# The head of a one-core S5 + SwiGLU kernel: other warm-up operands, a first tile in halves, reordered gate quarters, later parameter transposes

## The chip, the core and the metric

The kernel runs on one core of one Trainium2 chip. The metric is the device time of an execution in microseconds. The engines are called as in the profile: PE is TensorE (matmuls; PEld its weight loads), DVE is VectorE, ACT is ScalarE, POOL is GpSimd, SP is SyncE, which issues nearly all DMAs here. L712 means line 712 of the kernel before.

## The reference

For x of shape (1, 2048, 512) in bfloat16:

```python
xn = layernorm(x)                                  # over the last axis, eps 1e-5
# A: a diagonal complex state space model with 512 states
dt = exp(log_dt); Lam_bar = exp(dt * (Lambda_re + 1j * Lambda_im))
Bu = xn @ (((Lam_bar - 1) / Lam)[:, None] * B).T
h[t] = Lam_bar * h[t - 1] + Bu[t]                  # 2048 steps
y = 2 * real(h @ C.T) + xn * Dskip
# B: a feed-forward layer of width 1376
f = (silu(xn @ w_gate) * (xn @ w_up)) @ w_down
out = x + y + f
```

## The kernel before

The 2048 rows of x are 16 tiles of 128 rows; four tiles make a chunk, and there are four chunks. For each chunk the kernel normalizes the tiles (bn_stats, bn_aggr and the addition of eps on DVE, rstd by a power on POOL, and the scaling on DVE for chunks 0 and 1, on ACT for 2 and 3), transposes them into xnT so that the features lie on the partitions, and then runs matmuls: gate and up projections of the feed-forward layer in 11 column tiles of 128 (the last has 96), the B projection of the state space model, and at the end the down projection together with C and the Dskip term in one PSUM accumulation. The recurrence is turned into a real scan on DVE by tables of sines and cosines, which ACT and DVE make once in the head (`tables`, lines 635 to 649) from the parameters (`params_a`, `params_b`).

Only the head matters here. Tiles 0 to 3 are transposed on PE (`xt_tile_fine`, L523) and copied from PSUM to xnT by ACT (L529). Each of the other chunks is transposed by a DMA. So that PE can start before all four tiles are there, chunk 0's first six gate tiles are computed in quarters (`ffn_gate_quarters`, L712): for each row tile q four matmuls of 128 columns for each of the six gate tiles, 24 per quarter, and all six results stay in PSUM until the four quarters are done. After that come the up projections (L684) in matmuls of 512 columns.

In front of that PE runs ten warm-up matmuls of 512 columns on a tile of zeros, `zt`, which POOL sets (`pe_warm`, L451, L442), and four small transposes that bring the four parameter rows (`prow`) onto the partitions (`params_t`, L460). DVE copies the result to `praw` (L463); from it POOL computes dt as a power (L586), DVE the angle thn (L588), and ACT the first table step tm (L635), after which the sine tables follow.

What sets the order: the kernel lists its steps as tasks with what they read and write, and `_schedule` writes down a fixed order for each engine before anything runs. On PE and SP the order is that in which the tasks were added. On DVE, ACT and POOL it is a list scheduler with estimated durations (`est`): of the tasks that could begin within 200 ns of the earliest, it takes the one with the longest remaining path, plus a task's `prio`. `_plan` and `_emit` then put semaphore waits in front of the instructions; an engine runs its list strictly in order. Dependences follow the tasks' reads and writes, a later writer of a buffer waiting for its readers too.

The eight PSUM banks are handed out in a circle by `next_bank`; a bank is skipped only if PE wrote it last and no reader has been listed yet:

```python
def _bank_live(b):
    lw = g.last_w.get(("bk", b, 0))
    rd = g.readers.get(("bk", b, 0), ())
    return lw is not None and lw.eng == "pe" and len(rd) == 0 and not lw.name.startswith("pe_warm")
```

The loads go out on SP in the order x0, x1, x2 with x3, wgA (gate tiles 0 to 2), wg0 (gate tiles 3 to 5), wu0, wg1, wu1, x4 to x7. The four parameter rows are loaded on ACT's queue.

Of the kernel before, what the change touches and what calls it, by code (L numbers as in the profile page):

```python
# [21 lines left out]
    warm=10,  # L22
# [8 lines left out]
class _Task:  # L31
    __slots__ = ("eng", "fn", "deps", "name", "est", "idx", "dma", "sem", "lvl",
                 "waits", "nsig", "vc", "out", "lat", "bl", "start", "fin", "nbytes", "prio", "ninst")
# [5 lines left out]
class _Graph:  # L39
# [5 lines left out]
    def add(self, eng, fn, reads=(), writes=(), name="", est=100.0, dma=False, after=(), out=False, nbytes=0, prio=0.0, ninst=1):  # L45
        t = _Task()
        t.eng, t.fn, t.name, t.est, t.dma, t.out, t.nbytes, t.prio = eng, fn, name, float(est), dma, out, nbytes, prio
        t.ninst = ninst
        t.idx = len(self.tasks)
        deps = set(after)  # L50
        for r in reads:
            w = self.last_w.get(r)
            if w is not None:
                deps.add(w)
        for r in writes:
            w = self.last_w.get(r)
            if w is not None:
                deps.add(w)
            for rd in self.readers.get(r, ()):
                deps.add(rd)  # L60
        for r in reads:
            self.readers[r].append(t)
        for r in writes:
            self.last_w[r] = t
            self.readers[r] = []
        deps.discard(t)
        t.deps = deps
        t.sem = None
        t.lvl = 0
        t.lat = 0.0  # L70
        self.tasks.append(t)
        return t
# [8 lines left out]
def _schedule(tasks, engines, slack=200.0):  # L81
    succ = defaultdict(list)
    for t in tasks:
        for d in t.deps:
            succ[d].append(t)
    chain_next = {}
# [6 lines left out]
    for t in reversed(tasks):  # L93
        b = 0.0
        for s in succ[t]:
            if s.bl > b:
                b = s.bl
        v = b + t.est + t.lat
        cn = chain_next.get(t)
        if cn is not None and cn.bl + t.est > v:  # L100
            v = cn.bl + t.est
        t.bl = v + t.prio
    remaining = {e: [t for t in tasks if t.eng == e] for e in engines}
    nun = {t: len(t.deps) for t in tasks}
# [135 lines left out]
def bass_parallel_sum__ssm_conv_s5__swiglu_ffn__prompt_kernel(  # L240
# [32 lines left out]
    with es:  # L273
        block = es.enter_context(nc.Block())

        def sb(name, shape, dt):
            return es.enter_context(nc.sbuf_tensor(name, shape, dt))
# [48 lines left out]
        zt = sb("zt", [128, 512], B16)  # L326
# [80 lines left out]
        pload("ld_dskp", 3, A_Dskip)  # L407
        dma("ld_x0", x_sb[:, 0:1, :], x_v[:, 0:1, :], [("x", 0)], TILEB)
        dma("ld_x1", x_sb[:, 1:2, :], x_v[:, 1:2, :], [("x", 1)], TILEB)
        dma("ld_x2", x_sb[:, 2:4, :], x_v[:, 2:4, :], [("x", 2), ("x", 3)], 2 * TILEB)  # L410
        FQ = 3 * 128
        dma("ld_wgA", wg[:, :, 0:FQ], wg_v[:, :, 0:FQ], [("wg", "a")], 512 * FQ * 2)
        dma("ld_wg0", wg[:, :, FQ:FH0], wg_v[:, :, FQ:FH0], [("wg", 0)], 512 * (FH0 - FQ) * 2)
# [28 lines left out]
        g.add("pool", lambda e: e.memset(zt[:], 0.0), writes=[("zt",)], name="zt", est=450)  # L442
# [3 lines left out]
        def pe_warm(n):  # L446
            bk = next_bank()

            def mm(e, bk=bk):
                for _ in range(n):  # L450
                    inst = e.matmul(pbank[:, bk, :], lhsT=zt[:, 0:128], rhs=zt[:], start=True, stop=True)  # L451
                return inst
            g.add("pe", mm, reads=[("zt",)], writes=BK(bk), name="pe_warm", est=n * 430, ninst=n)

        def params_t():
            slot = next_tr()

            def tr(e, slot=slot):
                for k in range(4):
                    inst = e.transpose(out=ptr[:, slot, 4 * k:4 * k + 4], in_=prow[0:4, k, :], identity=ident[0:4, 0:4])  # L460
                return inst
            g.add("pe", tr, reads=[("prow", k) for k in range(4)] + [("ident",)], writes=BK(slot), name="parT", est=400, ninst=4)
            g.add("dve", lambda e, slot=slot: e.tensor_copy(out=praw[:].rearrange("p k a -> p (k a)"), in_=ptr[:, slot, 0:16]),  # L463
                  reads=BK(slot), writes=[("praw", k) for k in range(4)], name="parTev", est=80, prio=5000.0)
            for kt in range(KT):
                g.add("dve", lambda e, kt=kt: e.tensor_scalar(out=diagD[:, kt, :], in0=ident[:], scalar1=praw[:, 3, kt:kt + 1], scalar2=None, op0=ALU.mult),
                      reads=[("praw", 3), ("ident",)], writes=[("diagD", kt)], name="diagD%d" % kt, est=90)

        ln_prev = [None]
        ln_xn = {}  # L470

        def ln_tile(a, norm_act):
            g.add("dve", lambda e, a=a: e.bn_stats(out=st[:, a, :], in_=x_sb[:, a, :]),  # L473
                  reads=[("x", a)], writes=[("st", a)], name="bnst%d" % a, est=640,
                  after=(((ln_prev[0],) if (ln_prev[0] is not None and a < 4) else ()) + ((ln_xn[a - 2],) if (a < 4 and (a - 2) in ln_xn) else ())))
            g.add("dve", lambda e, a=a: e.bn_aggr(out=mv[:, a, :], in_=st[:, a, :]),
                  reads=[("st", a)], writes=[("mv", a)], name="bnag%d" % a, est=90)
            ln_prev[0] = g.add("dve", lambda e, a=a: e.tensor_scalar(out=ve[:, a:a + 1], in0=mv[:, a, 1:2], scalar1=EPS, scalar2=None, op0=ALU.add),  # L478
                                reads=[("mv", a)], writes=[("ve", a)], name="ve%d" % a, est=70)
            g.add("pool", lambda e, a=a: e.tensor_tensor(out=rstd[:, a:a + 1], in0=ve[:, a:a + 1], in1=mhalf[:, a:a + 1], op=ALU.pow),  # L480
                  reads=[("ve", a), ("mhalf",)], writes=[("rstd", a)], name="rstd%d" % a, est=400)
# [4 lines left out]
            else:  # L486
# [3 lines left out]
                      reads=[("x", a), ("rstd", a), ("nmr", a)], writes=[("xn", a % NXN)], name="xn%d" % a, est=710)  # L490

# [4 lines left out]
        def xt_chunk(c):  # L496
            a0 = 4 * c
            for pair in range(2):
# [12 lines left out]
                def evac(e, aa=aa, slot=slot):  # L511
# [3 lines left out]
                      writes=[("xnT", c % 2, aa % 4), ("xnT", c % 2, aa % 4 + 1)], name="xTev%d" % aa, est=930)  # L515

        def xt_tile_fine(c, a):
            if True:
                slot = next_tr()

                def tr4(e, a=a, slot=slot):
                    for kt in range(KT):
                        inst = e.transpose(out=ptr[:, slot, kt * 128:(kt + 1) * 128],  # L523
                                           in_=xn_sb[:, a % NXN, kt * 128:(kt + 1) * 128], identity=ident[:])
                    return inst
                g.add("pe", tr4, reads=[("xn", a % NXN), ("ident",)], writes=BK(slot), name="xT%d" % a, est=4 * 64, ninst=4)

                def evac(e, a=a, slot=slot):
                    return e.activation(out=xnT[:, c % 2, a % 4, :, :],  # L529
                                        in_=ptr[:, slot, 0:512].rearrange("p (k t) -> p k t", k=KT), func=AF.Identity)  # L530
                g.add("act", evac, reads=BK(slot), writes=[("xnT", c % 2, a % 4)], name="xTev%d" % a, est=500)

        def xt_chunk_dma(c):
            s0 = (4 * c) % NXN
            dma("xTd%d" % c, xnT[:, c % 2].rearrange("p j k t -> p (j k) t"), xn_sb[:, s0:s0 + 4, :],
                [("xnT", c % 2, j) for j in range(4)], 4 * TILEB, reads=[("xn", s0 + j) for j in range(4)], xpose=True)
# [140 lines left out]
        def ffn_mm(c, i, which):  # L677
# [9 lines left out]
            g.add("pe", mm, reads=[wres("wg" if which == "g" else "wu", i)] + [("xnT", c % 2, j) for j in range(4)],  # L687
# [12 lines left out]
        def ffn_gate_quarters(c, tiles):  # L700
            xt_tile_fine(c, 4 * c)
            banks = {i: next_bank() for i in tiles}
            for q in range(4):
                for ii, i in enumerate(tiles):
                    if q < 3 and ii == 0:
                        xt_tile_fine(c, 4 * c + q + 1)
                    fs = fsz[i]
                    bk = banks[i]

                    def mm(e, bk=bk, i=i, fs=fs, c=c, q=q):  # L710
                        for kt in range(KT):
                            inst = e.matmul(pbank[0:fs, bk, q * 128:(q + 1) * 128], lhsT=wg[:, kt, i * 128:i * 128 + fs], rhs=xnT[:, c % 2, q, kt, :],  # L712
                                            start=(kt == 0), stop=(kt == KT - 1))
                        return inst
                    g.add("pe", mm, reads=[wres("wg", i), ("xnT", c % 2, q)], writes=BK(bk), name="mm_gq%d_%d_%d" % (c, i, q), est=4 * 62, ninst=4)
# [29 lines left out]
        def ssm_b_unit(c, pt):  # L745
            br, bi = next_bank(), next_bank()
            for ri, bk in ((0, br), (1, bi)):
# [5 lines left out]
                g.add("pe", mm, reads=[("BT", ri, kt) for kt in range(KT)] + [("xnT", c % 2, j) for j in range(4)],  # L753
# [66 lines left out]
        def dc_chunk(c, mid=None, split_last=False):  # L820
# [10 lines left out]
            for (lt, c0, nc_), bk in zip(items, banks):  # L831
# [11 lines left out]
                g.add("pe", mmA, reads=[("hT", hb, i) for i in range(FT)] + [("wd", 0), ("wd", 1)] + ([("xnT", c % 2, lt)] + [("diagD", kt) for kt in range(KT)] if dg else []),  # L843
# [27 lines left out]
        ln_chunk(0)  # L871
        params_t()
# [7 lines left out]
        ffn_gate_quarters(0, [0, 1, 2, 3, 4, 5])  # L880
# [93 lines left out]
```

## Time and profile before

| | us |
|---|---|
| median of 3 runs | 183.49 (183.48 to 183.89) |
| span of the profiled execution, first to last instruction | 181.8 |
| median less span, what lies around it | 1.69 |
| PE busy | 177.7 (98% of the span) |
| DVE busy | 165.0 (91%) |
| ACT busy | 91.4 (50%) |
| POOL busy | 13.4 (7%) |

The profile gives the profiled execution by its span; its own time is taken as that span and the 1.69 us that separate the span from the median of the runs. The spans are of one execution. A row of the chain of waits or of the timeline gives the start, the length, the engine, the line, and in the timeline the operation, out<-in by the program's names, shapes, a count, and in brackets the idle time before it and what ended that. Matmuls are pipelined: their lengths overlap, and the distance of their starts is what one costs in a row.

### The profile page before, as it was taken

What the parts mean: (1) busy time and instruction counts of PE and PEld (TensorE: products, weight loads), DVE (VectorE), ACT (ScalarE), POOL (GpSimd) and SP (SyncE); (2) the same over time, 40 slices, a digit from 0 to 9 for tenths busy, and PEclk for the clock granted to TensorE, in tenths of its full rate; (3) what the DMA queues carried; (4) which work ended last, traced back from release to release, by engine and by line L of the source; (5) the groups of instructions that cost most, each with busy time, mean ns of one, the idle gap of its engine ahead of it and who ended that gap; (6) DMA issues with size and microseconds to landing.
All of it is one profiled execution on the core that took longest, in us unless ns stands there. A gap on an engine that the chain in (4) does not pass through costs nothing.

```text
span 181.8 us, 2579 instructions
## 1 busy us (share of the span) xinstructions
PE 177.7 (98%) x937; PEld 86.8 (48%) x937; DVE 165.0 (91%) x359; ACT 91.4 (50%) x162; POOL 13.4 (7%) x30
## 2 busy tenths in 40 slices
PE   6999999999999999999999999999999999999994
PEld 2694444444444454444444455444444444444643
DVE  3899878999999998999999999999999999999733
ACT  3299989996899108057666380026677620000000
POOL 5530500000000013000000220000000000000000
DMA  5992666669100000730000000620000000000102
GB/s 146 325 375 61 141 130 108 145 182 346 49 0 4 0 0 0 128 108 0 0 0 0 0 4 0 115 94 22 0 4 2 2 0 0 0 32 29 58 29 87
DMA packets 23388, 12.39 MB, mean 68 GB/s; under 512 B 15088, under 2 KB 23376, under 8 KB 23376
## 3 DMA queue, kind: packets, MB, share of 16 engines
q1 hardware_dynamic: 23344, 12.23, 25.3%
q8 instruction: 7, 0.11, 0.3%
q14 instruction: 5, 0.04, 0.1%
q10 hardware_dynamic: 32, 0.00, 0.0%
HBM read 6.46 MB, written 2.10 MB: 47 GB/s over the span
## 4 chain that ended last, share of the span: by engine, by line
PE 97%; ACT 0%; POOL 0%; DVE 0%; issue 0%; DVEq 0%; POOLq 0%
PE pb L684 39%; PE pb L838 21%; PE pb L854 15%; PE pb L750 15%; PE pb L712 3%; PE pb L451 2%; PE pb L841 1%; PE pb L523 1%; ACT xnT L529 0%; POOL zt L442 0%; DVE osb L865 0%; PE pb L460 0%; POOL mhalf L432 0%; DVEq L234 0%; POOLq L959 0%
## 5 line engine op out<-in xcount | busy, mean ns | idle before, releaser
L684 PE MATMUL pb<-xnT,wu 128*128 128x512 bf16 (+1 forms) x176 | 43.7, 379 | 0.0
L838 PE MATMUL pb<-wd,hT 128*128 128x512 bf16 (+3 forms) x187 | 39.7, 367 | 0.0
L789 DVE TENSOR_TENSOR_SCAN vq<-sm,car,vq 128x512 bf16<-128x512 f32 x32 | 39.5, 1271 | 0.1
L684 PE MATMUL pb<-xnT,wg 128*128 128x512 bf16 (+1 forms) x152 | 38.4, 379 | 0.0
L734 ACT ACTIVATE uf<-pb 128x512 bf16<-128x512 f32 (+1 forms) x44 | 25.4, 603 | 6.8 <-PE pb L684 6.6
L854 PE MATMUL pb<-W,hss 128*128 128x512 bf16 (+1 forms) x136 | 28.3, 366 | 0.0
L750 PE MATMUL pb<-xnT,BT 128*128 128x512 bf16 x128 | 28.1, 379 | 0.0
L684 PEld LDWEIGHTS pb<-xnT,wu 128*128 128x128 bf16 (+1 forms) x176 | 17.6, 100 | 20.1
L838 PEld LDWEIGHTS pb<-wd,hT 128*128 128x128 bf16 (+1 forms) x187 | 18.0, 98 | 18.5
L697 ACT ACTIVATE sg<-pb 128x512 bf16<-128x512 f32 (+1 forms) x38 | 22.5, 597 | 7.5 <-PE pb L684 7.4
L684 PEld LDWEIGHTS pb<-xnT,wg 128*128 128x128 bf16 (+1 forms) x152 | 15.3, 100 | 17.6
L757 ACT ACTIVATE u_sb<-pb 128x512 bf16<-128x512 f32 x16 | 9.6, 600 | 20.5 <-PE pb L750 20.3
L854 PEld LDWEIGHTS pb<-W,hss 128*128 128x128 bf16 x136 | 13.2, 98 | 13.9
L750 PEld LDWEIGHTS pb<-xnT,BT 128*128 128x128 bf16 x128 | 12.5, 98 | 15.1
L736 DVE TENSOR_TENSOR hT<-sg,uf 128x512 bf16<-128x512 bf16 (+1 forms) x44 | 18.1, 416 | 1.2 <-ACT uf L734 0.7
L480 POOL TENSOR_TENSOR rstd<-ve,mhalf 128x1 f32<-128x1 f32 x16 | 9.4, 604 | 90.4 <-DVE ve L478 90.4
L473 DVE BATCH_NORM_STATS2 st<-x_sb 128x6 f32<-128x512 bf16 x16 | 10.4, 685 | 2.9 <-DMA x_sb<-in_A_x_dram 2.8
L780 DVE TENSOR_TENSOR scrA<-u_sb,cosT 128x1024 bf16<-128x1024 bf16 x16 | 10.9, 682 | 0.7 <-ACT u_sb L759 0.7
L489 ACT ACTIVATE xn_sb<-x_sb,nmr,rstd 128x512 bf16<-128x512 bf16 x8 | 5.9, 803 | 10.2 <-POOL rstd L480 8.8
L799 DVE TENSOR_TENSOR scrA<-vq,sin 128x1024 bf16<-128x1024 bf16 x16 | 11.0, 684 | 0.0
L783 DVE TENSOR_TENSOR scrA<-u_sb,sin 128x1024 bf16<-128x1024 bf16 x16 | 10.9, 684 | 0.0
L795 DVE TENSOR_TENSOR scrA<-vq,cosT 128x1024 bf16<-128x1024 bf16 x16 | 10.9, 684 | 0.0
(71 smaller groups left out, 135.8 us busy)
## 6 DMA issues: line engine op xcount, KB each, us to landing
out_dram<-osb SPq DMA_DIRECT2D x15, 128.0 KB, 1.7
x_sb<-in_A_x_dram SPq DMA_DIRECT2D x3, 512.0 KB, 7.6
wd<-in_B_w_down_dram SPq DMA_DIRECT2D x1, 1280.0 KB, 7.0
wg<-in_B_w_gate_dram SPq DMA_DIRECT2D x2, 384.0 KB, 4.6
wu<-in_B_w_up_dram SPq DMA_DIRECT2D x1, 768.0 KB, 7.4
wg<-in_B_w_gate_dram SPq DMA_DIRECT2D x1, 608.0 KB, 8.5
wu<-in_B_w_up_dram SPq DMA_DIRECT2D x1, 608.0 KB, 9.6
x_sb<-in_A_x_dram SPq DMA_DIRECT2D x2, 128.0 KB, 2.2
```

Of the source, the lines that this page charges most:

```text
L684: inst = e.matmul(pbank[0:fs, bk, :].rearrange("p (j t) -> p j t", j=4), lhsT=w[:, kt, i * 128:i * 128 + fs], rhs=xnT[:, c % 2, :, kt, :], ...
L697: g.add("act", lambda e, sl=sl, bk=bk, fs=fs: e.activation(out=sg[0:fs, sl, :], in_=pbank[0:fs, bk, :], func=AF.Silu), reads=BK(bk), write ...
L734: g.add("act", lambda e, ul=ul, bk=bk, fs=fs: e.activation(out=uf[0:fs, ul, :], in_=pbank[0:fs, bk, :], func=AF.Identity), reads=BK(bk), w ...
L736: g.add("dve", lambda e, sl=sl, ul=ul, fs=fs, i=i, hb=hb: e.tensor_tensor(out=hT[0:fs, hb, i, :], in0=sg[0:fs, sl, :], in1=uf[0:fs, ul, :] ...
L750: inst = e.matmul(pbank[:, bk, :].rearrange("p (j t) -> p j t", j=4), lhsT=BT[:, ri, kt, pt * 128:(pt + 1) * 128], rhs=xnT[:, c % 2, :, kt ...
L780: g.add("dve", lambda e, sl=sl, U=U, Cb=Cb: e.tensor_tensor(out=pr2[:, sl, 0], in0=U, in1=Cb, op=ALU.mult), reads=ru + rdt, writes=[("pr", ...
L783: g.add("dve", lambda e, sl=sl, Usw=Usw, S2=S2: e.tensor_tensor(out=pr2[:, sl, 1], in0=Usw, in1=S2, op=ALU.mult), reads=ru + rdt, writes=[ ...
L789: g.add("dve", lambda e, sl=sl, ri=ri, pt=pt, rr=rr, c=c: e.tensor_tensor_scan(out=vq[:, sl, 1, ri, :], data0=rr[:, pt:pt + 1].to_broadcas ...
L795: g.add("dve", lambda e, sl=sl, Q=Q, Cb=Cb: e.tensor_tensor(out=po2[:, sl, 0], in0=Q, in1=Cb, op=ALU.mult), reads=rq + rdt, writes=[("po", ...
L799: g.add("dve", lambda e, sl=sl, Qsw=Qsw, S2sw=S2sw: e.tensor_tensor(out=po2[:, sl, 1], in0=Qsw, in1=S2sw, op=ALU.mult), reads=rq + rdt, wr ...
L838: inst = e.matmul(pbank[:, bk, 0:nc_], lhsT=hT[0:fs, hb, i, lt * 128:(lt + 1) * 128], rhs=wd[0:fs, i, c0:c0 + nc_], start=(i == 0), stop=F ...
L854: inst = e.matmul(pbank[:, bk, 0:nc_], lhsT=hss[:, hb, pt, ri, lt * 128:(lt + 1) * 128], rhs=W12[:, ri, pt, c0:c0 + nc_], start=False, sto ...
```

## The change

The warm-ups are nine and read a constant of ones (bfloat16) that the program's header sets on POOL in any case; `zt` and its memset are gone. x2 and x3 are loaded apart, x3 after wgA. The four parameter transposes are split into three (k = 0, 1, 2) and one (k = 3, Dskip, with diagD behind it) and stand inside the gate quarters. Tile 0 is transposed and copied in two halves of two transposes each, in two banks, and its first three gate tiles are computed in two halves to match. Three small matmuls (`pe_fill`) are put in front of them. The quarters run in another order, with gate tiles 0 to 2 (A) and 3 to 5 (B) apart. The order of the layer norm on DVE for tiles 0 to 3 is written out by hand in `ln_head` as order-only dependences (`order`, `odeps`), which the scheduler honours without a semaphore; rstd of the first four tiles has a higher `prio` and a larger `est`. `XN(c, j)` names the two halves of a transposed tile, `XNC(c)` all of a chunk. The computation is the same.

```diff
-    warm=10,
+    warm=9,
...
-        dma("ld_x2", x_sb[:, 2:4, :], x_v[:, 2:4, :], [("x", 2), ("x", 3)], 2 * TILEB)
+        dma("ld_x2", x_sb[:, 2:3, :], x_v[:, 2:3, :], [("x", 2)], TILEB)
         dma("ld_wgA", wg[:, :, 0:FQ], wg_v[:, :, 0:FQ], [("wg", "a")], 512 * FQ * 2)
+        dma("ld_x3", x_sb[:, 3:4, :], x_v[:, 3:4, :], [("x", 3)], TILEB)
         dma("ld_wg0", wg[:, :, FQ:FH0], wg_v[:, :, FQ:FH0], [("wg", 0)], 512 * (FH0 - FQ) * 2)
...
-        g.add("pool", lambda e: e.memset(zt[:], 0.0), writes=[("zt",)], name="zt", est=450)
...
+        def one_c(n):
+            return nc.const_aps.tensor(1.0, [128, n], B16)
...
         def pe_warm(n):
...
-                    inst = e.matmul(pbank[:, bk, :], lhsT=zt[:, 0:128], rhs=zt[:], start=True, stop=True)
+                    inst = e.matmul(pbank[:, bk, :], lhsT=one_c(128), rhs=one_c(512), start=True, stop=True)
...
+        def pe_fill(n):
+            bk = next_bank()
+
+            def mm(e, bk=bk):
+                for _ in range(n):
+                    inst = e.matmul(pbank[:, bk, 0:128], lhsT=one_c(128), rhs=one_c(128), start=True, stop=True)
+                return inst
+            g.add("pe", mm, writes=BK(bk), name="pe_warm_fill", est=n * 107, ninst=n)
...
-        def params_t():
+        def params_t(ks):
...
-                for k in range(4):
+                for k in ks:
                     inst = e.transpose(out=ptr[:, slot, 4 * k:4 * k + 4], in_=prow[0:4, k, :], identity=ident[0:4, 0:4])
...
-                  reads=[("ve", a), ("mhalf",)], writes=[("rstd", a)], name="rstd%d" % a, est=400)
+                  reads=[("ve", a), ("mhalf",)], writes=[("rstd", a)], name="rstd%d" % a, est=600, prio=(3000.0 if a < 4 else 0.0))
...
+        def ln_head():
+            for a in range(4):
+                ln_stats(a)
+            for a in range(4):
+                ln_scale(a, False)
+            seq = [ln_bn[0], ln_ag[0], ln_ve[0], ln_bn[1], ln_ag[1], ln_xn[0], ln_ve[1], ln_bn[2], ln_xn[1], ln_ag[2], ln_ve[2], ln_bn[3], ln_xn[2], ln_ag[3], ln_ve[3], ln_xn[3]]
+            for p, q in zip(seq, seq[1:]):
+                if p not in q.deps:
+                    q.odeps.add(p)
...
-        def xt_tile_fine(c, a):
+        def xt_tile_fine(c, a, parts=1):
+            n = KT // parts
+            for h in range(parts):
                 slot = next_tr()
+                k0 = h * n
...
+                g.add("act", evac, reads=BK(slot), writes=(XN(c, a % 4) if parts == 1 else [XN(c, a % 4)[h]]), name="xTev%d_%d" % (a, h), est=130 + 90 * n)
...
         def ffn_gate_quarters(c, tiles):
-            xt_tile_fine(c, 4 * c)
+            xt_tile_fine(c, 4 * c, parts=2)
             banks = {i: next_bank() for i in tiles}
-            for q in range(4):
-                for ii, i in enumerate(tiles):
-                    if q < 3 and ii == 0:
-                        xt_tile_fine(c, 4 * c + q + 1)
...
+            def quarter(q, ts, h0, h1):
+                for i in ts:
...
+            A, B = tiles[:3], tiles[3:]
+            pe_fill(3)
+            quarter(0, A, 0, 1)
+            quarter(0, A, 1, 2)
+            xt_tile_fine(c, 4 * c + 1)
+            params_t([0, 1, 2])
+            quarter(1, A, 0, 2)
+            quarter(0, B, 0, 2)
+            xt_tile_fine(c, 4 * c + 2)
+            quarter(1, B, 0, 2)
+            params_t([3])
+            quarter(2, A, 0, 2)
+            xt_tile_fine(c, 4 * c + 3)
+            quarter(2, B, 0, 2)
+            quarter(3, tiles, 0, 2)
...
         if _CFG["warm"]:
             pe_warm(_CFG["warm"])
-        ln_chunk(0)
-        params_t()
+        ln_head()
+        ffn_gate_quarters(0, [0, 1, 2, 3, 4, 5])
         params_a()
         tables()
         params_b()
...
         loads_stage_b2()
-        ffn_gate_quarters(0, [0, 1, 2, 3, 4, 5])
```

## The prediction

> **What bounds the kernel now.** I read the chain of waits first, in order of time, because it says which engine the end hangs on.
>
> ```profile
> 1.42 4.45 PE pb L451 x10
> 5.86 0.19 PE pb L460 x4
> 6.06 0.55 PE pb L523 x4
> 6.61 0.02 issue
> 6.63 0.61 ACT xnT L529
> 7.24 0.05 issue
> 7.29 1.59 PE pb L712 x24
> 8.87 0.22 PE pb L523 x4
> 9.09 1.34 PE pb L712 x24
> 10.43 0.22 PE pb L523 x4
> 10.66 2.68 PE pb L712 x48
> 13.34 13.81 PE pb L684 x64
> ...
> 172.35 6.94 PE pb L854 x40
> ```
>
> From 7.29 us to the end the chain lies on TensorE without a wait. Before that stand the warm-ups (L451), the parameter transposes (L460), the four transposes of the first x tile (L523) and its copy out of PSUM by ScalarE (L529). The busy times by stage agree: 5.90 of 5.90 us from 7.3 to 13.2, 152.08 of 152.10 from 27.2 to 179.3. So the time moves by as much as the first up-projection matmul moves, now 13.18 in the timeline, provided nothing later becomes late. Two covers keep that so: the DVE row that ends chunk 0's scan stage (the last hss write) ends at 64.8 and TensorE asks for it at 70.36, that of chunk 3 ends at 164.6 and is asked for at 172.35. I need only work out the head.
>
> Next, the timeline of the head, TensorE's and ScalarE's rows:
>
> ```profile
> 1.42 4.45 PE L451 MATMUL pb<-zt 128*128 128x512 bf16 x10 [1.42 <-POOL zt L442]
> ...
> 7.29 1.59 PE L712 MATMUL pb<-xnT,wg 128*128 128x128 bf16 x24
> ...
> 9.13 0.60 ACT L529 ACTIVATE xnT<-pb 128x512 bf16<-128x512 bf16 x1 [1.33 <-PE pb L523]
> ...
> 9.93 1.34 ACT L635 ACTIVATE scrC<-iot,sm 128x512 f32<-128x512 f32 x2 [0.20 <-DVE sm L588]
> ...
> 11.18 0.57 ACT L529 ACTIVATE xnT<-pb 128x512 bf16<-128x512 bf16 x1
> ```
>
> Prices from these. A 512-column warm-up costs 0.427 us (its starts run from 1.4 to 5.2), a 512-column matmul later 13.81/64 = 0.216: the clock doubles in between. A 128-column matmul costs (10.43 - 9.09)/24 = 0.056, and 0.107 (a quarter of 0.427) while the clock is low. The four transposes from 6.64 still lie 0.1 apart and the gates from 7.29 no longer do, so the clock rose at about 7.0, 5.6 us after the first warm-up. The third row is the one that matters most: the transposes of tile 2 begin at 8.71 and the copy starts at 9.13, 0.42 later; with its 0.60 and a hop of 0.06 (7.24 to 7.29), a tile can be used **1.08 us after its first transpose**. Now 24 gates (1.34 us) stand between each tile's transposes and its use, and tile 1's are done during tile 0's copy. That is why TensorE never waits after 7.29.
>
> Last, VectorE and GpSimd:
>
> ```profile
> 4.80 0.38 DVE L483 TENSOR_SCALAR xn_sb<-x_sb,mv,rstd 128x512 bf16<-128x512 bf16 x1
> ...
> 6.34 1.11 POOL L586 TENSOR_TENSOR sm<-ecst,praw 128x4 f32<-128x4 f32 x1 [0.46 <-DVE praw L463]
> ```
>
> Tile 0 is normalized at 5.18, yet its transposes start at 5.99, behind the warm-ups and the parameters: 0.8 us to be had. The power for dt takes 1.11 us where the planner counts 0.56.
>
> **The change, part by part.** *Warm-ups.* The wait for zt (till 1.42) goes; ACT, SP and POOL begin at 0.79, so TensorE can too (bounds 0.79 and 1.42). Nine then issue until 0.79 + 9 x 0.427 = 4.63 (5.26 at the late bound), so either way tile 0 is transposed when it is ready, at 5.18 + 0.05 = 5.23. Removing the memset saves POOL 0.5 us before 1.4 that nothing waits for.
>
> *Tile 0 in halves.* Two transposes at the low clock end 0.39 after the first starts (0.08 to the second, 0.31 long): 5.62, ScalarE at 5.66. No row shows a 256-column copy: between 0.21 (128x4, L443) and 0.60 (128x512); by columns 0.40. It ends at 6.06, TensorE can go at 6.12. The second half ends by 6.43, hidden.
>
> *The fill.* pe_fill takes the next bank, and by the rule of next_bank that is bank 1, which holds tile 0's first half. So it waits for that copy and stands between it and the first gate: 3 x 0.107 = 0.32 us (0.17 at the high clock). If the clock again rises 5.6 us after the first warm-up, at 6.4, the first gate is at **6.44** instead of 7.29: 0.85 gained.
>
> *New order.* Twelve gates of tile 0 (0.67) end at 7.11. Only now come tile 1's transposes (0.22), then three parameter transposes (0.09): TensorE is through at 7.42. But the next twelve gates need tile 1 at 7.11 + 1.08 = 8.19: **a wait of 0.77** that is not there now. Queued behind them in order are tile 0's other twelve gates, whose operands are there (wg0 lands 5.3 after its issue at 2.7, at 8.0, and is issued some 0.4 later at most, behind the same bytes). They run 8.86 to 9.53, when tile 2 is transposed; the next quarter and the Dskip transpose end at 10.45.
>
> *Tile 2's copy.* By transposes alone it would run 9.95 to 10.55, and TensorE would wait 0.16. But ScalarE's order is fixed by the planner. Followed by hand with its costs, the parameters' copy comes ahead of tile 2's normalization on VectorE, dt ahead of tile 3's rstd on POOL, and the two tm rows (L635) at 7.8 and 8.4 of planner time, ahead of tile 2's copy at 9.17. On the chip: parameters out of PSUM 7.59 to 7.75, dt 7.84 to 8.95, thn 9.0, the tm pair at 9.19 and 9.82, and the copy, 0.62 after that start as now, at 10.44. TensorE gets tile 2 at 11.10: **0.65 of wait**, not 0.16.
>
> *Tile 3.* Its transposes follow twelve gates at 11.77 and allow the copy at 12.19; the sine pair ahead of it (tile 3 normalized 10.0 behind dt and rstd, then 0.42, 0.69 and twice 0.53) lets it start at 12.25, so the data is there at 12.91 while TensorE is through at 12.66: **0.25**. The last 24 gates take 1.34: the up-projection starts at **14.25**.
>
> Sum against the profiled execution: first gate -0.85; tile 1's transposes now behind it +0.22; parameters behind it +0.12; waits 0.77 + 0.65 + 0.25 = +1.67; the 0.06 that the gates lost at 8.0 to wg0's landing (24 of them took 1.59 from 7.29, 1.50 from 8.93) -0.06. That is +1.10, or 1.07 by the walk (14.25 - 13.18), the walk being less rounded. *Loads:* SP issues one more 0.4 us descriptor; x2 comes earlier, x3 after wgA at about 6.1, before its statistics start at 6.65; cost nothing (if x3 came later than 7.3, tile 3 would follow, hidden until 8.0). SP's later transposes and the weights keep order and bytes. diagD moves later, needed at 62.3. The tables (tm) begin at 9.2 instead of 9.93, so ScalarE, busy 12.98 of 14.0 us up to 27.2, is not later against a TensorE that is.
>
> [...] The rise at 7.0 came in a stretch with 0.4 us of idle TensorE; the change leaves 0.6 (4.63 to 5.23) and 0.5 (5.62 to 6.12). [...]
>
> **Rivals.** [...]
>
> *The tm pair stands behind tile 2's copy.* Then the waits are 0.77 + 0.16 + 0.19 and the shift +0.53, with an early clock +0.35: **183.9**, within 0.3%. For it: the planner's times are its own and 0.2 us of slack can swap two steps. Against: by its figures the pair is issued 0.7 and more before the copy.
>
> *Faster: the copies are covered.* Then only the first gate counts: -0.85 + 0.34 for the moved transposes, and -0.06: **182.9**. It decides where the 1.08 us from transpose to use falls under the 0.31 of work behind tile 1's transposes. For it: the first gate surely comes earlier. Against: today's four copies took 0.57 to 0.60, none near 0.3.
>
> *The const is no earlier* (warm-ups at 1.42): clock at 7.0, six or seven gates more at 0.107, +1.3 to 1.4: 184.8; inside the range of the forecast.
>
> **How the numbers follow.** The span is 181.8 and the median of the runs 183.49; the 1.69 around it stays. 183.49 + 1.07 = **184.6**, likeliest (0.52, its own range 184.2 to 184.9: half copy 0.21 to 0.60, fill at either clock, const at either start). Late clock 0.18, tm behind 0.20, copies covered 0.10. Range 183.5 to 185.5: it takes in the first three and leaves out the faster case. A measurement of this kernel can tell about 0.3%, 0.55 us: faster 0.1, same 0.2, slower 0.7.
>
> **What would show it.** In the changed profile: warm-ups from 0.79; the first L712-like gate near 6.4 behind three short matmuls that ScalarE released; a wait of TensorE for xnT near 7.4, one near 10.5 with L635's pair ahead of the copy, a small one near 12.7; the first up matmul near 14.2; no idle time after. The forecast falls if the gates run through from the first to the up-projection, if tile 1's copy is out within 0.4 us, or if a new idle time appears behind 14.2.

## The result: 0.94 us slower, and the profile after

| us | before | after |
|---|---|---|
| median of 12 runs each | 183.49 | 184.43 |
| span of the profiled execution | 181.8 | 182.8 |
| warm-ups, first start | 1.42 | 0.82 |
| first gate matmul | 7.29 | 6.33 |
| first up-projection matmul | 13.18 | 14.15 |

The ratio of the runs is 1.0069, 95% interval 1.0040 to 1.0099; two executions near 187 raise it, the medians alone give 1.0051. Ten of the twelve executions of the changed kernel took 184.31 to 184.58 us, two took 186.81 and 187.06; these two were not profiled, but the experiments have profiles of executions that were as late.

TensorE's timeline of the changed kernel (start, length, line, operation, count, and in brackets the idle time before and what ended it; the lengths of matmuls overlap, a gate's is 0.22 us and the next starts 0.056 later, so starts are what counts):

```profile
0.82 4.00 PE L466 MATMUL pb<-const-bfloat16-1.0 128*128 128x512 bf16 x9 [0.82 <-PEq L1024]
5.28 0.51 PE L573 MATMUL pb<-ident,xn_sb 128*128 128x128 bf16 x4 [0.46 <-DVE ve L504]
6.15 0.34 PE L475 MATMUL pb<-const-bfloat16-1.0 128*128 128x128 bf16 x3 [0.36 <-ACT xnT L579]
6.33 0.83 PE L761 MATMUL pb<-xnT,wg 128*128 128x128 bf16 x12
7.00 0.39 PE L573 MATMUL pb<-ident,xn_sb 128*128 128x128 bf16 x4
7.32 0.23 PE L484 MATMUL pb<-ident,prow 4*128 4x4 bf16 x3
8.08 1.51 PE L761 MATMUL pb<-xnT,wg 128*128 128x128 bf16 x24 [0.53 <-ACT xnT L579]
9.43 0.39 PE L573 MATMUL pb<-ident,xn_sb 128*128 128x128 bf16 x4
9.65 0.83 PE L761 MATMUL pb<-xnT,wg 128*128 128x128 bf16 x12
10.42 0.17 PE L484 MATMUL pb<-ident,prow 4*128 4x4 bf16 x1
11.04 0.84 PE L761 MATMUL pb<-xnT,wg 128*128 128x128 bf16 x12 [0.45 <-ACT xnT L579]
11.72 0.39 PE L573 MATMUL pb<-ident,xn_sb 128*128 128x128 bf16 x4
11.94 2.37 PE L761 MATMUL pb<-xnT,wg 128*128 128x128 bf16 x36
14.15 1.03 PE L734 MATMUL pb<-xnT,wu 128*128 128x512 bf16 x4
```

Before, the rows from 7.29 on carried no bracket at all. Now two carry one, both released by ScalarE's copies of a transposed tile (L579). The fill (L475) waits for a copy too, and the gates stand behind it. A third wait is hidden in the row of 36 gates; the weight loads (PEld) show it, ahead of the last 24:

```profile
12.79 1.34 PEld L761 LDWEIGHTS pb<-xnT,wg 128*128 128x128 bf16 x24 [0.19 <-ACT xnT L579]
```

ScalarE's and GpSimd's rows of the same timeline show why the second wait is as long as it is:

```profile
7.42 0.60 ACT L579 ACTIVATE xnT<-pb 128x512 bf16<-128x512 bf16 x1 [1.06 <-PE pb L573]
...
7.82 1.11 POOL L636 TENSOR_TENSOR sm<-ecst,praw 128x4 f32<-128x4 f32 x1 [0.55 <-DVE praw L487]
...
9.17 1.34 ACT L685 ACTIVATE scrC<-iot,sm 128x512 f32<-128x512 f32 x2 [1.15 <-DVE sm L638]
...
10.41 0.57 ACT L579 ACTIVATE xnT<-pb 128x512 bf16<-128x512 bf16 x1
...
11.60 0.63 ACT L691 ACTIVATE sin<-scrC 128x512 bf16<-128x512 f32 x1 [0.43 <-DVE scrC L689]
...
12.14 0.60 ACT L579 ACTIVATE xnT<-pb 128x512 bf16<-128x512 bf16 x1
```

ScalarE idles 1.15 us, waiting for thn, does the tm pair, and only then copies tile 2, whose transposes began at 9.43. Tile 1's copy started 0.42 us after the tile's first transpose (7.00 to 7.42); at that rate tile 2's could have started at 9.85. It has no bracket, since its data was there and ScalarE was still at the tm pair. From the last 24 gates on the chain of waits lies on TensorE again, and TensorE has no wait behind them:

```profile
12.80 1.51 PE pb L761 x24
14.31 13.81 PE pb L734 x64
28.12 13.81 PE pb L816 x64
```

### The profile page after: what moved, and what is told of

Same layout as the page of the kernel before. It is cut to its first block, busy times and chain, and to the rows that moved or that the text cites. A ratio compares the mean times of both kernels' runs of the same rounds, so it can differ in the third digit from the quotient of the medians.

```text
span 182.8 us, 2579 instructions
## 1 busy us (share of the span) xinstructions
PE 177.2 (97%) x931; PEld 86.7 (47%) x939; DVE 165.4 (90%) x360; ACT 92.6 (51%) x163; POOL 13.0 (7%) x29
## 4 chain that ended last, share of the span: by engine, by line
PE 93%; DVE 2%; ACT 1%; DMA 1%; POOL 1%; issue 1%; DVEq 0%
PE pb L734 39%; PE pb L904 21%; PE pb L816 15%; PE pb L920 15%; PE pb L761 2%; DMA x_sb<-in_A_x_dram 1%; PE pb L907 1%; ACT scrC L685 1%; DVE st L500 1%; POOL sm L636 1%; ACT xnT L579 0%; PE pb L573 0%; DVE osb L931 0%; DVE mv L502 0%; PE pb L475 0%
## 5 line engine op out<-in xcount | busy, mean ns | idle before, releaser
L904 PE MATMUL pb<-wd,hT 128*128 128x512 bf16 (+3 forms) x181 | 38.9, 366 | 0.3
L800 ACT ACTIVATE uf<-pb 128x512 bf16<-128x512 f32 (+1 forms) x44 | 26.0, 600 | 16.8 <-DVE hT L802 8.7
L823 ACT ACTIVATE u_sb<-pb 128x512 bf16<-128x512 f32 x16 | 9.5, 593 | 21.8 <-PE pb L816 21.8
L920 PEld LDWEIGHTS pb<-W,hss 128*128 128x128 bf16 x136 | 13.2, 98 | 13.9
L825 ACT ACTIVATE u_sb<-pb 128x512 bf16<-128x512 f32 x16 | 9.6, 597 | 3.0 <-PE pb L816 2.4
```

The source lines that it names most:

```text
L800: g.add("act", lambda e, ul=ul, bk=bk, fs=fs: e.activation(out=uf[0:fs, ul, :], in_=pbank[0:fs, bk, :], func=AF.Identity), reads=BK(bk), w ...
L904: inst = e.matmul(pbank[:, bk, 0:nc_], lhsT=hT[0:fs, hb, i, lt * 128:(lt + 1) * 128], rhs=wd[0:fs, i, c0:c0 + nc_], start=(i == 0), stop=F ...
L920: inst = e.matmul(pbank[:, bk, 0:nc_], lhsT=hss[:, hb, pt, ri, lt * 128:(lt + 1) * 128], rhs=W12[:, ri, pt, c0:c0 + nc_], start=False, sto ...
```

## Experiments

All edits are to the changed kernel unless it says otherwise. "The change" is its median, 184.43 us. "Late" is an execution more than 1 us above its kernel's median; without its two late ones the change's median is 184.41. The traces differ by some tenths of a us in the start of the first gate (6.16 in e7_both, 6.33 in the change), so starts behind it are best compared from it on.

**Table steps behind tile 2's copy.**

```diff
+    order=((xt_ev[2],) if pt < 2 else ())   # of tm; xt_ev[2] is tile 2's copy
```

> The changed kernel, with one thing more: the first two table steps (tm) are put behind tile 2's copy in ScalarE's order. Theory A (a tile's copy is no longer covered by gates, and tile 2's copy stands behind the tm pair): the wait before the third pair of gate groups shrinks from 0.54 us to 0.1 to 0.3, the one before the last 24 gates stays near 0.2, so the first up-projection matmul comes at about 13.8 instead of 14.15 and the time falls by 0.3 to 0.45, to about 184.05. Rival B (the loss is the later first gates, the loads or the clock; ScalarE's order is of no account): no change, 184.4.

Measured: 184.29. The planner put the two small sines of the parameters into the gap instead, ahead of the copy:

```profile
9.48 0.30 ACT L633 ACTIVATE sm<-sm,halfpi 128x4 f32<-128x4 f32 x1 [1.55 <-DVE sm L628]
10.11 0.20 ACT L631 ACTIVATE sm<-sm 128x4 f32<-128x4 f32 x1 [0.34 <-DVE sm L624]
10.22 0.58 ACT L581 ACTIVATE xnT<-pb 128x512 bf16<-128x512 bf16 x1
```

The copy moved from 10.41 to 10.22, the third group from 11.04 to 10.86, the time by 0.14. Half of the move is there before the edit can act: the first gate came at 6.24 against 6.33. The direction is theory A's, the size is not, and 0.14 alone can't be told from no change (the executions overlap, 184.17 to 184.71 but for one late one). The edit did only part of what it was meant to do; the next run has the sines behind as well.

**The same, sines too.**

```diff
+    order=((xt_ev[2],) if pt < 2 else ())   # of tm
+    for t_ in g.tasks:
+        if t_.name in ("sin_" + tag, "cos_" + tag):
+            t_.odeps.add(xt_ev[2])
```

> The changed kernel, with all of the parameters' steps on ScalarE behind tile 2's copy (in e1_tm_behind the two small sines still stood ahead of it and kept it at 10.2). Order of the quarters as the change has it. Theory A: the wait for tile 1 stays at 0.53, the copy of tile 2 starts at 9.85 instead of 10.41, the third group at 10.5 instead of 11.04, the up-projection at 13.5 to 13.65, time 183.8 to 183.95; so of the 0.76 us that e7_both gained, 0.5 to 0.6 are ScalarE's order and 0.2 the order of the quarters. Rival F (the order of the quarters is needed too): 184.2 and more.

Measured: 183.92, so ScalarE's order alone is worth 0.5 us. Nine executions took 183.85 to 184.03, four of the 13 were late (186.74 to 187.01), and the profiled one (186.88) is among these. Its starts can't be set against the others, but it shows what a late execution is. The low clock lasts till about 13.1, and 24 gates take 2.74 us instead of 1.51:

```profile
9.00 2.74 PE L767 MATMUL pb<-xnT,wg 128*128 128x128 bf16 x24 [0.52 <-ACT xnT L581]
...
13.38 0.84 PE L767 MATMUL pb<-xnT,wg 128*128 128x128 bf16 x12
```

**The old order of the quarters.**

```diff
-            quarter(1, A, 0, 2)
             quarter(0, B, 0, 2)
+            quarter(1, A, 0, 2)
```

> The changed kernel, with tile 0's gates for gate tiles 3 to 5 put back ahead of tile 1's for gate tiles 0 to 2. Theory A: the wait for tile 1's copy goes, but the twelve gates wait for the parameters' copy out of the bank that they share (0.3 us, or more if the weights land after 7.8), and tile 2's copy still stands behind the tm pair, whose start has not moved, so the third group starts at 11.04 as before: time 184.4, no change. Rival B (the order of the quarters alone costs the time): 0.5 us less, 183.9.

Measured: 184.43, no change at all. TensorE's timeline:

```profile
7.73 1.50 PE L761 MATMUL pb<-xnT,wg 128*128 128x128 bf16 x24 [0.35 <-DVE praw L487]
...
10.05 0.17 PE L484 MATMUL pb<-ident,prow 4*128 4x4 bf16 x1
10.88 0.84 PE L761 MATMUL pb<-xnT,wg 128*128 128x128 bf16 x12 [0.65 <-ACT xnT L579]
```

The first wait turned into a shorter one for the parameters' copy out of the shared bank (L487). From the first gate on (6.17 here, 6.33 in the change) the second group came 0.19 earlier, and the third exactly as late, 4.71 us: what was won was given back in front of tile 2's copy, 0.65 of wait instead of 0.45.

**Both together.** The edits of e10_params_behind and e3_order_back.

> The changed kernel with both: tile 0's gates for gate tiles 3 to 5 back ahead of tile 1's for 0 to 2, and the tm pair and the two small sines of the parameters behind tile 2's copy on ScalarE. Theory A: the two waits that each hid the other's removal go together: the second gate group starts at 7.75, the third near 10.15 instead of 11.04, the last near 11.95, the up-projection near 13.3 instead of 14.15: 0.75 to 0.9 less than the change, 183.5 to 183.7. Rival B (loads or clock set the head): at most 0.2 less, 184.2 and more.

Measured: 183.67, 0.76 less than the change, where the parts give 0.51 and 0.00. The second wait is gone:

```profile
9.48 0.83 PE L767 MATMUL pb<-xnT,wg 128*128 128x128 bf16 x12
10.24 0.17 PE L484 MATMUL pb<-ident,prow 4*128 4x4 bf16 x1
10.35 0.84 PE L767 MATMUL pb<-xnT,wg 128*128 128x128 bf16 x12
```

Of the 0.94 us lost, 0.76 are thus these two orders; in this kernel the old order of the quarters is worth 0.25 once ScalarE's order no longer hides it. In the profiled execution (183.84, 0.17 above the median) the third group started at 10.35 instead of the 10.15 expected, since the second still waited 0.53 us, till 7.90 (the weights of gate tiles 3 to 5 landed at 7.86).

**No fill.**

```diff
-            pe_fill(3)
```

> The changed kernel without the three fill matmuls. Theory A: they stand between the first half copy and the first gate, so everything up to the parameters' copy and with it the tm pair comes 0.18 us earlier (3 x 0.06): first gate at 6.15, up-projection at 13.97, time 184.25. Rival B: they fill idle time and cost nothing: 184.4. Rival C: they keep the clock up: without them more executions near 187.

Measured: median 184.28; eight executions took 184.07 to 184.66, four 185.77 to 186.56. A came true: the median of the eight is 184.14, so the fill costs 0.2 to 0.3 us where the clock is up. C is not decided by this run: four late ones of 12 against two of 12 are too few to tell apart. The profiled execution (186.56) is a late one:

```profile
5.13 0.61 PE L573 MATMUL pb<-ident,xn_sb 128*128 128x128 bf16 x4 [0.31 <-DVE ve L504]
6.00 1.46 PE L761 MATMUL pb<-xnT,wg 128*128 128x128 bf16 x12 [0.26 <-ACT xnT L579]
...
8.58 2.74 PE L761 MATMUL pb<-xnT,wg 128*128 128x128 bf16 x24 [0.52 <-ACT xnT L579]
...
13.07 0.90 PE L761 MATMUL pb<-xnT,wg 128*128 128x128 bf16 x12
```

Twenty-four gates take 2.74 us where the change's take 1.51, and the rows return to their short lengths only after 13 us. The four are of two kinds: at 186.55 and 186.56 the granted clock of the whole execution is 1.00, as in the change's two, while at 185.77 and 185.90 it is 0.991. By an estimate from these figures 0.009 of 184 us is what 3.3 us at half clock would lose; no trace shows such an execution.

**Five warm-ups.**

```diff
-    warm=9,
+    warm=5,
```

> The changed kernel with five warm-ups instead of nine: TensorE idles from 2.9 to 5.2 us. [...] Rival D: median as the change has it, 184.4.

Measured: 186.84, so rival D's 184.4 did not come; all four executions took 186.49 to 187.01, which is where the change's two outliers lie. The profile shows the low clock until about 12.7:

```profile
0.82 2.29 PE L466 MATMUL pb<-const-bfloat16-1.0 128*128 128x512 bf16 x5 [0.82 <-PEq L1024]
5.24 0.61 PE L573 MATMUL pb<-ident,xn_sb 128*128 128x128 bf16 x4 [2.12 <-DVE ve L504]
...
9.01 2.74 PE L761 MATMUL pb<-xnT,wg 128*128 128x128 bf16 x24 [0.52 <-ACT xnT L579]
```

**A fill that does not wait, and one more warm-up.**

```diff
-        def pe_fill(n):
-            bk = next_bank()
+        def pe_fill(n, bk=0):     # bank 0 is the warm-ups'
...
-            pe_fill(3)
+            pe_fill(4)
...
-    warm=9,
+    warm=10,
```

> The changed kernel, with ten warm-ups and with the fill (four instead of three) written to the warm-ups' bank, so that it does not wait for the first half copy and runs while TensorE waits for it. Theory A (copies and their order set the head, and the clock rises late where TensorE idles around the first transposes): first gate near 6.0, everything to the up-projection 0.15 to 0.2 us earlier (about 13.97), median 184.2, and executions above 185 gone or rare (0 or 1 of 12, against 2 of 12 for the change and 4 of 12 without any fill). Rival D (the clock's rise depends on nothing that this kernel does): as many above 185 as the change has.

Measured: 184.30 (five executions, 184.15 to 184.65). The first gate came at 6.03, the up-projection at 13.85, a little earlier than expected; the median lies 0.13 below the change, and none of the five was late, which five executions alone could not show.

**The warm-ups alone, put into the kernel before.**

```diff
-    warm=10,
+    warm=9,
...
-        g.add("pool", lambda e: e.memset(zt[:], 0.0), writes=[("zt",)], name="zt", est=450)
...
-                    inst = e.matmul(pbank[:, bk, :], lhsT=zt[:, 0:128], rhs=zt[:], start=True, stop=True)
+                    inst = e.matmul(pbank[:, bk, :], lhsT=one_c(128), rhs=one_c(512), start=True, stop=True)
...
+            g.tasks[-1].deps.add(ln_r[0])   # dt stays behind the second rstd
```

> The kernel before, with only the warm-ups changed: nine, on the header's constant, no memset of zeros (and dt kept behind the second rstd on GpSimd, where it stands in the kernel before). Theory A: the warm-ups end at 4.6 instead of 5.7, but tile 1's transposes stand ahead of the gates and need tile 1 normalized at 6.6, and gate tiles 3 to 5 can't start before their weights land (8.0 in the kernel before): the gain is 0.05 to 0.3 us, time 183.2 to 183.45. Rival B (the first gate sets the head): 0.85 less, 182.65.

Measured: 184.36, with executions from 183.34 to 185.80. The five best (183.34 to 183.61) lie at theory A's time or just above it, hardly below the kernel before (183.48 in the same session). Theory A missed the median. Rival B is not tested: its 0.85 did not come, but in the profiled execution the first gate did not move by as much either (7.20 against 7.29). The warm-ups that begin earlier (0.81 against 1.42) also end earlier (4.81 against 5.87), and TensorE idles 0.65 us before tile 0's transposes; that this is the cause is likely, not shown. The five executions from 184.89 on have a granted clock of 0.991. In the profiled one (184.37, granted clock 1.00) the clock rose at about 9.4:

```profile
4.75 0.26 PE L462 MATMUL pb<-ident,prow 4*128 4x4 bf16 x4
5.66 0.61 PE L527 MATMUL pb<-ident,xn_sb 128*128 128x128 bf16 x4 [0.65 <-DVE ve L481]
6.80 0.61 PE L527 MATMUL pb<-ident,xn_sb 128*128 128x128 bf16 x4 [0.54 <-DVE xn_sb L487]
7.20 2.55 PE L717 MATMUL pb<-xnT,wg 128*128 128x128 bf16 x24
```

**All repairs of the change together**: e7_both with the free fill and ten warm-ups.

> e7_both with ten warm-ups and the free fill of e5_fill_free: all findings on the change together, its own order of the rest kept. Theory A: the 0.15 of e5_fill_free adds to the 0.76 of e7_both, unless the second gate group waits for its weights (they landed at 7.1 to 7.9): 183.45 to 183.7, and no execution above 185 (the change had 2 of 12, e7_both 1 of 12, e10_params_behind 4 of 13). Rival D (the clock does not depend on the fill): 1 to 4 of 12 above 185.

Measured: 183.42, eleven executions from 183.25 to 184.05, against 183.47 for the kernel before in the same session (ratio 0.9999, 0.9991 to 1.0008). From the first gate to the up-projection no row carries a bracket:

```profile
6.10 0.84 PE L766 MATMUL pb<-xnT,wg 128*128 128x128 bf16 x12
...
7.43 1.51 PE L766 MATMUL pb<-xnT,wg 128*128 128x128 bf16 x24
...
9.87 0.84 PE L766 MATMUL pb<-xnT,wg 128*128 128x128 bf16 x12
...
12.98 5.34 PE L739 MATMUL pb<-xnT,wu 128*128 128x512 bf16 x24
```

The loss is gone and none of the eleven is late; the kernel stands where it stood before the change. The change's other parts (loads, layer norm order, half tile, Dskip) are all still in it, so on balance they cost nothing; none was tried alone. Its first gate comes 1.19 us earlier than that of the kernel before, its up-projection only 0.20. The transposes and parameters that now lie behind the first gate take the rest, with two short waits that only the weight loads show: 0.20 us for the weights of gate tiles 3 to 5 and 0.19 for tile 3's copy.

**A head built anew.** Tile 1's transposes between the two halves of tile 0's first gates, each later tile transposed two groups ahead, the parameters behind tile 1's first group, dt behind the fourth rstd, tm behind tile 3's copy; ten warm-ups and the free fill:

```diff
             quarter(0, A, 0, 1)
+            xt_tile_fine(c, 4 * c + 1)
             quarter(0, A, 1, 2)
-            xt_tile_fine(c, 4 * c + 1)
-            params_t([0, 1, 2])
-            quarter(1, A, 0, 2)
             quarter(0, B, 0, 2)
             xt_tile_fine(c, 4 * c + 2)
+            quarter(1, A, 0, 2)
+            params_t([0, 1, 2])
             quarter(1, B, 0, 2)
...
```

> A head made from the findings: ten warm-ups and the free fill, tile 1's transposes between the two halves of tile 0's first gates, then tile 0's other gates, each later tile transposed two gate groups ahead of its use, parameters after tile 1's gates, dt behind the fourth rstd on GpSimd, tm behind tile 3's copy. Theory A: first gate at 6.0 and no wait but up to 0.4 us for the weights of gate tiles 3 to 5, up-projection at 12.4 to 12.7 instead of 13.18, time 182.7 to 183.0, below both kernels. Rival E (the tables, now 0.9 us later, hold up TensorE behind the head): a new idle time after 13 us and 183.5 or more.

Measured: 184.34, theory A missed; the time and a new idle time are those that rival E named, but what TensorE waits for are loads. TensorE's waits in the profile (what waited <- for what: total, times, longest):

```profile
PE pb L765 <- DMA wg<-in_B_w_gate_dram: 1.1, 2, 0.8
PE pb L820 <- DMA xnT<-xn_sb: 0.6, 1, 0.6
```

With the copies covered the weights are late: the first gate waited for them till 6.54, the second group till 7.91, and the up-projection came at 13.53. These weights landed at 6.40 and 7.87; in the other traces it was 5.64 to 6.17 and 7.11 to 7.98, so part of this is the one execution. Far behind the head, at 78 us, the transposing load of the third chunk is late. It was issued at 73.08, against 71.31 in the next kernel, which puts the parameters early and has no such wait; that the late parameters are the cause is likely, but only argued.

**The same idea with the parameters early.** Order: first half of tile 0, tile 1's transposes, second half, parameters, tile 1's A group, tile 2's transposes (into bank 1), the two B groups, Dskip, tile 3's transposes, the rest; ScalarE as in e10_params_behind.

> A second head from the findings, which keeps the parameters early (in e8_rebuilt a transposing load of the third chunk came late): ten warm-ups and the free fill, tile 1's transposes between the halves of tile 0's first gates, parameters, tile 1's gates for gate tiles 0 to 2, tile 2's transposes, then the gates of tiles 0 and 1 that need the later weights, tile 3's transposes, the rest; the tm pair and the small sines behind tile 2's copy. Theory A (uncovered copies, ScalarE's order, weights): first gate 6.0 to 6.5 (weights land 5.6 to 6.4), one wait of 0.4 us for tile 1, up-projection at 12.6 to 13.0 instead of 13.18 before the change, time 182.9 to 183.3, no idle time later. Rival E (later table steps hold up TensorE behind the head): 183.5 or more with a new idle time.

Measured: 183.96, theory A missed and rival E's time came. The gates had only 0.2 us of wait left, and the up-projection could have begun at 13.15, but its first matmul, at 13.76, waited for the first silu to empty the bank that it writes:

```profile
PE pb L739 <- ACT sg L793: 0.5, 1, 0.5
PE pb L766 <- ACT xnT L580: 0.2, 1, 0.2
```

The silu stood behind a sine step on ScalarE, started at 12.50 after 0.97 us of idle time. It is the change's own fault once more: a table step put ahead of a step that TensorE waits for.

**And that step behind the second silu.**

```diff
+    order=((xt_ev["silu1"],) if pt == 0 else ())   # of the first sine pair
```

> e9_two_ahead with the first sine pair (L641, L643 of the kernel before) put behind the second silu on ScalarE: in e9_two_ahead the second up-projection's bank waited 0.47 us for a silu that stood behind that step. Theory A: this wait goes, the up-projections run on from 13.15 without idle time and the time is 183.3 to 183.5, about that of the kernel before: nothing much below it is to be had from the order of the head alone, since the gates, from 6.0 to 6.3 on, take 6.3 us and the transposes between them 0.5. Rival E (the tables are late now): a new idle time behind the head and 183.8 or more.

Measured: 183.27, eleven executions from 183.16 to 183.56; the up-projection starts at 12.93. (The wait of 0.47 that the expectation names was, by the trace, that of the first up-projection for the first silu; the edit puts both silus ahead of the sines.) Against the kernel before the ratio is 0.9991 (0.9982 to 1.0000): 0.2 us below it by the medians, less than the 0.3% that a measurement was taken to tell. Against the change it is 1.16 us.

## Why the prediction was right, point by point

*What bounds.* The time moved by what the first up-projection matmul moved: 0.97 in the traces, 0.94 in the medians. (The spans of the two profiled executions differ by 1.01; the change's, at 184.58, is the slowest of its ten.) Nothing behind the head became late.

*The walk.* Forecast and measured starts: first gate 6.44 and 6.33, second group 8.19 and 8.08, third 11.10 and 11.04, last 24 gates 12.91 and 12.80, up-projection 14.25 and 14.15. The 0.11 at the first gate is the clock, and here the prediction had a step wrong: it let the rise come 5.6 us after the first warm-up, at 6.4. It came at 5.55, between tile 0's transposes (0.51 for the four, 0.61 where it is low), so the fill cost 0.18 instead of 0.32. No such distance is fixed: it is 4.73 us in the change and about 8.6 in e4_warm_only (9.4 less 0.81), and in e3_order_back the rise falls into the warm-ups (nine take 3.55 us there, 4.00 in the change). That the error stayed small is luck. The half copy took 0.38 (estimate 0.40), warm-ups began at 0.82 (0.79).

*The first wait*, 1.08 us from transposes to use against 0.3 us of work: 7.00 to 8.08 in the trace, 1.08. The row's bracket has 0.53 where the forecast has 0.77, for two reasons: the parameter transposes began 0.1 later than reckoned, and a bracket counts from where the last matmul ends, not from where the next could start. The end of the wait is the same, since the copy sets it. *The second*: dt at 7.82 (7.84), tm at 9.17 (9.19), copy at 10.41 (10.44). That these hit closer than the first gate did is two errors that cancel, the gate 0.11 early and the parameters 0.1 late behind it. The time of e10_params_behind and the trace of e7_both, where tile 2's copy starts 0.42 after its first transpose (9.26 to 9.68), show that this order is the cause. *The third* was 0.18 instead of 0.25. The forecast let the sine pair hold the copy back, and that term was wrong: one of the pair (L691) and a small cosine (L631) stood ahead, but the copy began 0.42 after its tile's first transpose (11.72 to 12.14), as with nothing in front of it. The wait is the same 1.08 (11.72 to 12.80) as the first.

*Loads.* They cost nothing, as said: the weights of gate tiles 3 to 5 landed at 7.11 instead of 8.0 or later, ahead of their use at 8.76. They become the bound once the copies are covered (e7_both, e8_rebuilt).

*The rivals.* The clock that comes late exists: the traces of e2_no_fill, e6_warm5 and e10_params_behind show it, and by their times two of the change's twelve executions had it, against a chance of 0.18. Its price was wrong: the range ends at 185.5, and 186.8 to 187.1 was measured. The 185.5 is my estimate, which let the low clock end at about 10.4. No run shows that; the three traces show the low clock till 12.7 to 13.2, and all three have a wait of 0.52 us in the middle. The tm pair behind the copy was priced at 183.9; e10_params_behind, which makes it so, took 183.92. The early clock in that price is in the change's trace, where the fill cost 0.18 instead of 0.32. "The copies are covered" was priced at 182.9; e11_silu_first comes nearest, at 183.27: it still waits 0.2 us for a copy twice. Its first weights landed at 5.97, so the first gate could have come at most 0.2 us before its 6.17.

*What the change did right* is in the runs too: the first gate came 0.96 us earlier, with the warm-ups earlier, the parameters out of the way and the first tile in halves. The order behind it gave back 1.9.

## What to carry to other kernels

Before moving work to an earlier start, ask what the moved work was covering: 24 gates hid every copy here, and a group of 12 can't hide 1.08 us. An engine that feeds the bottleneck through a fixed order must not have a step in front of the feed that waits for something slow; here a list made from estimated durations put it there. The estimate of 0.56 us for a step of 1.11 is at most part of the reason: worked through the kernel's own planner with 1.11, one of the two tm steps still stands ahead of the copy (no run tried it). And when two waits stand in a row, undoing the first alone can show nothing (0.00 us here, 0.51 for the second alone, 0.76 together), so undo both before a theory is dropped.

## What the runs showed of the hardware that was not expected

Executions of the same kernel differ by more than 2 us: ten of the change's twelve took 184.31 to 184.58, two 186.81 and 187.06. The profiled one of the change (184.58) has the clock's rise at 5.55, ahead of the gates; the profiled late ones (e2_no_fill, 186.56, and e10_params_behind, 186.88) have it at about 13. That the late ones without a profile missed it too is inferred from their times. How often an execution is late differs with what TensorE does around the first transposes. Late executions, by more than 1 us above the kernel's median: 10 of 61 in the five kernels with nine warm-ups and the waiting fill (the change, e1, e3, e7, e10); 4 of 12 with no fill; none of 45 in those with ten warm-ups and the free fill (e5, e8, e9, e11, e12); of the kernel before, 2 of 35 in the session of the first experiments and none of 62 in the three others. With five warm-ups all four lie 2 us and more above the change. Which of the two, the tenth warm-up or the free fill, does it was not separated, and four of those five kernels also have another order than the change.

Up to the first gate TensorE idles twice by 0.3 to 0.5 us in the profiles of the five with the waiting fill (0.85 once in e3_order_back, where the clock rose during the warm-ups, by their 3.55 us), and at most 0.3 at a time in those with the free one (0.8 in e8_rebuilt, where the clock had risen before: tile 0's transposes took 0.40). These lengths alone do not decide: the profile of e10_params_behind is late with 0.41 and 0.26, that of the change early with 0.46 and 0.36.

The low clock is read here from the distance of matmuls: 24 gates take 2.74 us where it is low (e2_no_fill, e6_warm5, e10_params_behind) and 1.51 where it is up (the change). The granted clock of the views is no help in the head: it reads 1.00 from 0.8 to 5.0 us in the change, where the warm-ups lie 0.427 apart. The trace of the change has a record of the clock from 5.55 on, that of the kernel before has none. In the others the rise is estimated from the starts of the gates, by the two distances, 0.107 and 0.056: about 9.4 in e4_warm_only (24 gates from 7.20 take 2.55 us), 12.7 in e6_warm5 (12 gates from 11.97 take 1.17) and 13.1 in e10_params_behind (12 gates from 11.96 take 1.39), where 24 and 12 take 1.51 and 0.83 at the full clock.

What brings the rise on is left open; no run settles it. In e6_warm5 TensorE worked from 6.1 us with one wait of 0.52, and the rise came at about 12.7; in e4_warm_only it came at about 9.4, behind waits of 0.65 and 0.54 that ended at 5.66 and 6.80. Transposes run faster once the clock is up: tile 0's four took 0.40 us in e3_order_back (from 5.22) and 0.61 in e1_tm_behind (from 5.19).
